# Two PSUM banks for the first head pair's later scores, and an earlier hand-over of the bank of useless matmuls

## The chip, the cores and the metric

The kernel runs on one core of a Trainium2 chip. The core has five engines with queues of their own: TensorE (PE in the profile), VectorE (DVE), ScalarE (ACT), GpSimd (POOL) and SyncE (SP), which issues the DMAs. Matmuls write PSUM, the small memory of eight banks that PE accumulates in. The metric is device microseconds of one execution.

## The reference

Three layers in a row, in float32, on 4 batches of 576 positions:

```python
# attention: 8 heads of 64, window 128, ALiBi
scores = scale * q @ k.T - slope * |rel|      # where 0 <= rel < 128
attn   = softmax(scores);  x = attn @ v       # heads side by side: [4, 576, 512]
# gated MLP, the "mixture" below
h = gelu(x @ w_in);  u, v = h[..., :512], h[..., 512:]
v = layernorm(v) * g_ln
x = x + (u * (w_sg @ v + b_sg)) @ w_out
# channel mix
xk, xr = mix(x, x_prev, mu_k), mix(x, x_prev, mu_r)
r = sigmoid(xr @ w_r)
out = r * (relu(xk @ w_k) ** 2 @ w_v)
```

## The kernel before

**Stages.** The attention works on 16 pairs of heads, one pair a "slot". The first four pairs are batch 0; from then on the mixture of batch b and the attention of batch b+1 are merged, and the channel mix (with a Strassen-like scheme of products `qa`, `qb`, `qd`, `vps` and the gate's products `rps`) comes last. Matmuls of the mixture and the last stage are split in high and low parts, three passes for one product.

**A slot of the attention.** A pair's 576 rows are nine tiles of 64. `s_items` (L920) takes two banks for four tiles of scores; `s_bank` (L960) records 16 small matmuls (`s<-rawqk`) for them, and `s_tile` (L989) for each tile a reduce on DVE (L996, adds the mask, gives `p` and `nmax`) and an exp on ACT (L619). `s_last` does the ninth tile, number 8, in a bank of the same ring and calls `tail_tile` (L937): `sum`, reciprocal `rin`, and `p` of tile 8 times `rin`. `t_step` (L1018) transposes `p` on PE (`tf`), 13 transposes a pair, of which the last step needs tile 8. `av_step` (L1061) forms `rt` (`rin` spread over rows, on PE) and the product `a<-pf,rawv`; `slot(c)` (L1105) strings together the scores of pair c and the product of pair c-1. The masks are multiples of the first head pair's mask (`mask_pair`); this first mask is made on DVE from `rel`, which POOL makes. The pattern `tri` is built by POOL and completed by two DVE copies.

**Banks.** PSUM is in three rings: `psS` (2 banks, tag `s`: scores), `psT` (2 banks: transposes, `rt`), and `psD` (4 banks, tag `d`: products of the mixture, and a bank `wps` that useless matmuls write). A tile of a ring waits until all users of the tile that many places before it are done.

**Useless matmuls.** `filler` (L734) offers up to 150 matmuls of a mask with itself (128x384, bf16) into `wps`, between a first and a last one. The planner queues one of them wherever PE has nothing ready in its plan; so they stand where the plan had PE idle, and on the chip they run in their place in the queue whether PE had waited or not. `filler_end` sets the last one, and what it waits for.

```python
    def filler_end(self, out, l, r, late):

        o = self.r.fill[-1][2] = self.mm([(out, l, r, True, True, {})])
        o.deps.add(late)
```

**Mixture work among the first slots.** `v_first` (L1176) puts products with the first parts of `w_in` into three `psD` banks from slot 2 on. `job` (L809) decodes `w_in`: ACT (L818), a shift on DVE (L708), a shift-and-or on DVE (L691, `wdec<-st,wdec`), then a high part (a cast, on ACT, DVE or POOL) and a low part (a subtract, on DVE or POOL).

**Order of the work.** All operations are recorded first. `schedule` (L430), a list scheduler with estimated costs, then fixes each engine's order and, for an operation with several engines allowed, the engine. A table `PRI` shifts the latest start of a group of operations and a table `ENG` biases the choice of its engine; both are written-out numbers.

Of the kernel before, what the change touches and what calls it, by code (L numbers as in the profile page):

```python
# [61 lines left out]
    ("rawv0", "sp"): -145256, ("rel", "pool"): -60569, ("rin", "dve"): -25233, ("rin.0", "dve"): 5257, ("rin.1", "dve"): -69646,  # L62
    ("rl.c", "act"): -82948, ("rl.c", "act/dve/pool"): -108272, ("rps", "pe"): -153964, ("rps.a", "pe"): 16695, ("rps.c", "pe"): 41240,
    ("rr.v", "dve"): -87265, ("rr.v", "sp"): -128743, ("rr.w", "dve"): -349494, ("rr.w", "sp"): -12240, ("rr.x", "sp"): -22703,
    ("rr.z", "sp"): 157296, ("rs.c", "act"): -44771, ("rsd", "sp"): -282416, ("rsd.a", "sp"): -190365, ("rsd.c", "sp"): -14632,
# [3 lines left out]
    ("tri", "pool"): 10322, ("u", "dve"): 58110, ("u.1", "dve"): 3031, ("u.3", "dve"): 136950, ("v", "dve"): 21613, ("v", "dve/pool"): 318339,  # L69
    ("v.1", "dve"): 13625, ("v.1", "dve/pool"): -47891, ("v.3", "dve"): -107478, ("v.3", "dve/pool/act"): -242645, ("vhl", "act/dve/pool"): 69188,  # L70
    ("vhl", "dve"): -218606, ("vhl", "dve/pool"): -323701, ("vhl.1", "act/dve/pool"): -20746, ("vhl.1", "dve"): -190493,
    ("vhl.1", "dve/pool"): 83593, ("vhl.3", "act/dve/pool"): 132502, ("vhl.3", "dve"): -196785, ("vhl.3", "dve/pool"): 167692,
    ("vps.v", "pe"): -32792, ("vps.w", "pe"): -206906, ("vps.x", "pe"): 92350, ("vps.z", "pe"): -226565, ("vsg", "dve"): -174379,
    ("vsg", "dve/pool"): 661483, ("vsg.1", "dve"): -26065, ("vsg.1", "dve/pool"): 26297, ("vsg.3", "dve"): -156326, ("vsg.3", "dve/pool"): -8209,
    ("vx", "act/dve"): -74444, ("vx.1", "act/dve"): -40169, ("vx.3", "act/dve"): -16277, ("w7", "act/dve/pool"): -810863,
    ("w7", "dve/pool"): 172733, ("w7.3", "act/dve/pool"): -178636, ("w7.3", "dve/pool"): -226904, ("w7.a", "act/dve/pool"): 19037,
    ("w7.a", "dve/pool"): -40750, ("w_in_t.0", "act/dve/pool"): 27024, ("w_in_t.0", "dve/pool"): 182778, ("w_in_t.u", "act/dve/pool"): 36136,
    ("w_in_t.u", "dve/pool"): 25486, ("w_out_t.o", "act/dve/pool"): -233990, ("w_out_t.o", "dve/pool"): 184889, ("w_r_t.3", "act/dve/pool"): 13396,
    ("w_r_t.3", "dve/pool"): -60043, ("w_sg_t.1", "act/dve/pool"): 929461, ("w_sg_t.1", "dve/pool"): -163370, ("w_v7.w", "act/dve/pool"): -179176,
# [676 lines left out]
def attn_gmlp_rwkv_kernel(  # L756
# [1100 lines left out]
```

## Time and profile before

| | |
|---|---|
| three runs, us | median 559.45 (559.27 to 560.44) |
| the profiled execution, us | 559.52 |
| its span, first to last instruction, us | 557.80 (1.72 lie around it) |
| PE busy | 548.5 us, 98% |
| DVE, ACT, POOL busy | 476.5 us (85%), 347.8 us (62%), 236.5 us (42%) |
| granted TensorE clock | 1.00 in every slice |

How to read the rows further down: a row of the timeline gives the start, the length and the work of one run of equal instructions on an engine, and in brackets how long the engine was idle ahead of it and what ended that. PE runs matmuls pipelined, so their modelled lengths overlap by up to some 0.2 us; what counts is from start to start. A useless matmul is a row `wps<-mask`, `wps<-w_out_t` or `wps<-wk`.

### The profile page before, as it was taken

The numbers are of one execution on the slowest core, as the hardware profiler recorded it, in microseconds if no ns is written. First come the engines' busy times: TensorE is split into PE (matmuls) and PEld (weight loads), VectorE is DVE, ScalarE is ACT, GpSimd is POOL, SyncE is SP. The second block draws the span as 40 slices with busy tenths as digits, with TensorE's granted clock in tenths as the row PEclk, the third lists the DMA queues.
The fourth block names the chain that finished last, engine by engine and source line by source line (L and its number), as shares of the span: only waits on it lengthen the run. The fifth ranks groups of instructions, "written<-read, shape, count | busy, mean of one in ns | idle before, by whom it ended". The sixth has DMA issues, their size and how long they took to land. (4 is left out here: it accounts for less than half of the span.)

```text
span 557.8 us, 12880 instructions
## 1 busy us (share of the span) xinstructions
PE 548.5 (98%) x4594; PEld 492.5 (88%) x4594; DVE 476.5 (85%) x1195; ACT 347.8 (62%) x925; POOL 236.5 (42%) x382
## 2 busy tenths in 40 slices
PE   8999999999999999999999999999999999999997
PEld 4777799988999888899899989898999978799997
DVE  6999998888988889887999999987958986659994
ACT  5998987649866687572554469876565663326240
POOL 4674735837645448472466203311431422024531
PEclk9999999999999999999999999999999999999999
DMA  8864334355432453334722276738545597644623
GB/s 274 326 184 125 112 124 143 94 205 166 125 125 84 154 172 104 114 86 125 248 93 60 73 255 204 241 89 271 167 156 203 191 313 244 211 131 164 215 77 132
DMA packets 54896, 91.79 MB, mean 165 GB/s; under 512 B 6832, under 2 KB 32944, under 8 KB 54320
## 3 DMA queue, kind: packets, MB, share of 16 engines
q1 hardware_dynamic: 54832, 90.97, 50.3%
q8 instruction: 36, 0.59, 0.4%
q14 instruction: 28, 0.23, 0.1%
HBM read 62.10 MB, written 28.84 MB: 163 GB/s over the span
## 5 line engine op out<-in xcount | busy, mean ns | idle before, releaser
L619 ACT ACTIVATE p<-p,nmax 128x192 f32<-128x192 f32 (+2 forms) x144 | 61.6, 430 | 16.1 <-DVE nmax L996 15.5
L597 PE MATMUL d<-w_sg_t,vhl 128*128 128x288 f32 x448 | 63.9, 298 | 0.4 <-DVE u L691 0.4
L597 PEld LDWEIGHTS d<-w_sg_t,vhl 128*128 128x128 f32 x448 | 60.1, 188 | 2.2 <-issue 1.7
L597 PE MATMUL d<-xg,w_in_t 128*128 128x288 f32 x384 | 56.6, 298 | 0.0
L597 PEld LDWEIGHTS d<-xg,w_in_t 128*128 128x128 f32 x384 | 53.0, 188 | 3.5 <-issue 1.7
L597 PE MATMUL d<-gg,w_out_t 128*128 128x288 f32 x384 | 55.7, 298 | 0.2 <-POOL gg L644 0.2
L597 PEld LDWEIGHTS d<-gg,w_out_t 128*128 128x128 f32 x384 | 52.3, 188 | 2.1 <-issue 1.1
L597 PE MATMUL rps<-w_r_t,xr 128*128 128x512 f32 x216 | 51.6, 391 | 1.0 <-ACT rs L619 1.0
L597 PE MATMUL d<-w_in_t,xg 128*128 128x512 f32 x192 | 50.9, 400 | 0.1
L597 PEld LDWEIGHTS rps<-w_r_t,xr 128*128 128x128 f32 x216 | 40.3, 188 | 9.2 <-ACT rs L619 1.4
L996 DVE CUSTOM_DVE_ANT_0 p<-s,mask 128x192 f32<-128x192 f32 (+1 forms) x144 | 40.3, 326 | 5.0 <-PE s L597 4.6
L597 PE MATMUL vps<-w_v_t,k 128*128 128x256 f32 (+1 forms) x252 | 43.2, 329 | 0.1
L597 PEld LDWEIGHTS vps<-w_v_t,k 128*128 128x128 f32 x252 | 37.8, 190 | 4.7 <-DVE rr L642 0.5
L597 PEld LDWEIGHTS d<-w_in_t,xg 128*128 128x128 f32 x192 | 34.1, 188 | 6.8 <-issue 1.4
L644 POOL TENSOR_TENSOR k2o<-k2o,rr 128x256 f32<-128x256 f32 x13 | 16.9, 1305 | 46.7 <-DVE k2o L642 46.6
L619 ACT ACTIVATE gt<-gt 128x288 f32<-128x288 f32 (+2 forms) x52 | 26.6, 515 | 14.8 <-DVE gt L691 14.7
L597 PE MATMUL s<-rawqk 64*64 64x192 f32 (+2 forms) x576 | 33.5, 318 | 0.6 <-DVE tri L632 0.6
L597 PEld LDWEIGHTS a<-pf,rawv 64*64 64x64 f32 (+1 forms) x832 | 26.9, 135 | 5.1 <-DVE v L691 1.5
L644 POOL TENSOR_TENSOR vsg<-vsg,u 128x288 f32<-128x288 f32 x25 | 23.1, 928 | 18.6 <-DVE vsg L691 18.0
L597 PE MATMUL a<-pf,rawv 64*64 64x64 f32 (+2 forms) x832 | 30.0, 239 | 0.9 <-DVE v L691 0.9
L691 DVE SCALAR_TENSOR_TENSOR gt<-gt,d 128x288 f32<-128x288 f32 (+2 forms) x52 | 27.5, 534 | 2.8 <-ACT gt L619 2.5
L658 POOL TENSOR_SCALAR_AFFINE_SELECT pf<-pf 128x128 f32<-128x128 f32 (+1 forms) x61 | 23.5, 418 | 14.7 <-ACT pf L630 13.4
(237 smaller groups left out, 1373.2 us busy)
## 6 DMA issues: line engine op xcount, KB each, us to landing
rawqk<-in_qk_dram SPq DMA_DIRECT2D x15, 576.0 KB, 4.9
k2d<-e SPq DMA_DIRECT2D x36, 192.0 KB, 2.5
k2f<-k2d SPq DMA_DIRECT2D x16, 384.0 KB, 5.4
xc<-xs SPq DMA_DIRECT2D x7, 770.0 KB, 5.1
rawv<-in_v_dram SPq DMA_DIRECT2D x32, 160.0 KB, 3.3
wx<-wx SPq DMA_DIRECT2D x40, 128.0 KB, 3.1
xs<-x SPq DMA_DIRECT2D x4, 1154.0 KB, 4.7
rr<-rsd SPq DMA_DIRECT2D x18, 256.0 KB, 3.6
```

Source lines behind the costliest of these rows:

```text
L597: pe.matmul(real(o), real(l), real(r), start=st, stop=sp, **ex)
L619: nc.scalar.activation(real(out), real(in_), func, scale=scale, **kw)
L644: alts.append(("pool", 140 + 2.12 * out.n, lambda: nc.gpsimd.tensor_tensor(real(out), real(a), real(b), op)))
L658: self.nc.gpsimd.affine_select(out=out, in_=in_, pattern=[[0, v.ids.shape[1]], [0, 2], [sgn, 64]], compare_op=cmp, fill=0.0, base=64 * sgn ...
L691: alts.append(("dve", cost or self._dve(out.n, False, isinstance(s, Vw)), lambda: nc.vector.scalar_tensor_tensor(real(out), real(a), real( ...
L996: K.raw("dve", 70 + w / 0.96, lambda: nc.vector.tensor_tensor_reduce(out=real(po), in0=real(s), in1=real(ma), scale=-0.125, scalar=3.0e38, ...
```

## The change

Three edits. (1) Pair 0's second four tiles of scores go to two banks of `psD` in place of `psS`. (2) The bank `wps` of useless matmuls ends at the start of slot 2 (it ended after the fourth product `a`), and its successor `wps2` is taken right behind the three `psD` tiles of `v_first`, in front of slot 2. So the ring `psD` is used in the order `wps`, `s`, `s`, then three mixture tiles, `wps2`, where it was `wps`, three mixture tiles, `wps2`. (3) Every number of `PRI` and `ENG` is new.

```diff
 PRI = {
-    ("a", "pe"): -9616, ("a.0", "pe"): 43767, ("a.1", "pe"): -320743, ("bm", "dve"): -606882, ...
+    ("a", "pe"): -90488, ("a.0", "pe"): 9130, ("a.1", "pe"): 20578, ("bm", "dve"): -844676, ...
...
     def s_items(c, half):
-        banks = [T("psS", [P, 2, 256], F32, "s") for _ in range(2)]
+        banks = [T("psS", [P, 2, 256], F32, "s") if c or not half else T("psD", [P, 2, 256], F32, "d", "s") for _ in range(2)]
         return banks, [x for k in range(2) for o in range(2) for x in s_item(c, 4 * half + 2 * k + o, banks[o], k)]
...
     for n in range(5):
         if n == 0:
             K.filler(wps[:, 0:384], *warm)
+        if n == 2:
+            K.filler_end(wps[:, 0:384], *warm[:2], next(o for o in reversed(R.ops) if o.pe))
         if n > 1:
             v_first(range(n - 2, n - 1))
+        if n == 2:
+            wps2 = T("psD", [P, 512], F32, "d", "wps")
+            K.filler(wps2[:, 0:384], *warm)
...
-    K.filler_end(wps[:, 0:384], *warm[:2], AV[3])
-    wps2 = T("psD", [P, 512], F32, "d", "wps")
-    K.filler(wps2[:, 0:384], *warm)
     for b in range(B):
```

The new order of each engine, where the prediction speaks of it. Line numbers of the changed kernel are one lower.

The useless matmuls on PE, counted from the two orders (each is a pair of rows, `LDWEIGHTS mask` and `MATMUL wps<-mask`):

| stretch of PE's queue | before | changed |
|---|---|---|
| ahead of the first product `a` | 16 | 21 |
| from the first to the second `a` | 9 | 1 |
| from the second to the fifth `a` | 6 | 10 |
| the last one on `mask`, behind the fifth | 1 | 1 |
| entry of the last stage, on `w_out` / on `wk` | 14 / 20 | 18 / 15 |
| all | 66 | 66 |

The first slot on DVE. `mask<-rel` is the first mask, `mask<-mask` those of other pairs, the ISA rows the reduces with their `nmax`, `tri` the pattern. Before:

```order
L708 TENSOR_SCALAR mask_145<-rel_115 64x192 x4
L708 TENSOR_SCALAR mask_145<-mask_145 128x384 x3
L632 COPY tri_158<-tri_158 128x256
L996 ISA p_147,nmax_186<-s_169,mask_145 128x64
L996 ISA nmax_186 128x1
L996 ISA p_147,nmax_190<-s_172,mask_145 128x128
L996 ISA nmax_190 128x1
L996 ISA p_195,nmax_196<-s_169,mask_145 128x192
L996 ISA nmax_196 128x1
L996 ISA p_195,nmax_201<-s_172,mask_145 128x192
L996 ISA nmax_201 128x1
L632 COPY tri_158<-tri_158 128x256
```

Changed:

```order
L707 TENSOR_SCALAR mask_151<-rel_132 64x192 x4
L707 TENSOR_SCALAR mask_151<-mask_151 128x384 x2
L995 ISA p_115,nmax_180<-s_164,mask_151 128x64
L995 ISA nmax_180 128x1
L995 ISA p_115,nmax_183<-s_167,mask_151 128x128
L995 ISA nmax_183 128x1
L995 ISA p_189,nmax_190<-s_164,mask_151 128x192
L995 ISA nmax_190 128x1
L995 ISA p_189,nmax_195<-s_167,mask_151 128x192
L995 ISA nmax_195 128x1
L631 COPY tri_154<-tri_154 128x256 x2
L995 ISA p_222,nmax_223<-s_207,mask_151 128x192
```

One of the three other masks is gone (POOL makes it), and both copies of `tri` stand behind the first four reduces, in a row. On POOL three memsets of `p` now stand ahead of `rel`, and that mask stands between the memset of `tri` and the six selects that complete it; behind the copies DVE has the five reduces of tiles 4 to 8 in a row, as before.

PE between the first and the second product `a` (pair 1's tail, pair 2's first scores). Before, seven pairs of useless matmuls like the first two rows stand ahead of these, and ahead of them eight `tf` and eight `s`:

```order
L741 LDWEIGHTS mask
L741 MATMUL wps<-mask 128x384
L605 MATMUL tf<-ident,p 128x128 x5
L597 MATMUL s<-rawqk 64x192 x8
L741 LDWEIGHTS mask
L741 MATMUL wps<-mask 128x384
L597 MATMUL rt<-ident,rin 64x64 x16
L597 MATMUL a<-pf,rawv 64x128 x6
```

Changed:

```order
L596 MATMUL s<-rawqk 64x192 x2
L604 MATMUL tf<-ident,p 128x128 x4
L596 LDWEIGHTS mask
L596 MATMUL wps<-mask 128x384
L604 MATMUL tf<-ident,p 128x128 x4
L596 MATMUL s<-rawqk 64x64 x2
L596 MATMUL s<-rawqk 64x128 x2
L596 MATMUL s<-rawqk 64x192 x4
L604 MATMUL tf<-ident,p 128x128 x5
L596 MATMUL s<-rawqk 64x192 x8
L596 MATMUL rt<-ident,rin 64x64 x16
L596 MATMUL d<-w_in_t,xg 128x512 x3
L596 MATMUL a<-pf,rawv 64x128 x6
```

The run of eight useless matmuls is gone; one is left, the last of its bank, and the next bank's first comes later than this piece. The first three products of the mixture, `d<-w_in_t,xg`, stand ahead of the second `a` (they stood behind it).

ACT at the end of the gate's products (`rs<-rps` are the gate's six last results). Before:

```order
L630 CAST w_v_t<-k2o 128x2x256
L619 ACTIVATE rs<-rps 128x512 x2
L630 CAST w_v_t<-k2o 128x2x256
L630 CAST k_6487<-k2f 128x768
L630 CAST k_6610<-k2f 128x768
L619 ACTIVATE rs<-rps 128x512
L630 CAST w_v_t<-k2o 128x2x256
L619 ACTIVATE rs<-rps 128x512 x2
```

Changed:

```order
L618 ACTIVATE rs<-rps 128x512 x2
L629 CAST w_v_t<-k2o 128x2x256
L629 CAST k_6617<-k2f 128x768
L629 CAST w_v_t<-k2o 128x2x256
L1404 ACTIVATE e<-e 128x384
L1405 ACTIVATE e<-e 128x384
L618 ACTIVATE rs<-rps 128x512 x2
L629 CAST w_v_t<-k2o 128x2x256
L618 ACTIVATE rs<-rps 128x512
```

Ahead of the fourth `rs` there were two casts `k<-k2f`, whose input comes by DMA; there is now one, and an operation pair on `e` and one more cast of `w_v_t`. In SP's queue the two loads `k2f` for these casts come right behind the four loads `k2o`, and ahead of the last stores `k2d<-e`; they came behind these stores.

On DVE all eight subtracts of the `w_in` decode (128x512, L644 on POOL before) stand in its queue now, seven of them ahead of the scores of pair 3's last tile. Ahead of the same place DVE has one more cast and two more copies of `rt`, one `p` by `rin` and one shift-and-or more, and one copy of `pf` and one mask less. ACT has four casts of `w_in`, two copies of `rt` and one `p` by `rin` less there, and one cast of `w_sg` and two of `xg` more. In pair 1's tail DVE goes from tile 8's reduce to `p<-p,rin` over one subtract, `sum`, an add for `x`, `rin` and a shift; before, over one shift-and-or, `sum`, `rin` and two reduces of pair 2.

## Rows read from the trace of the kernel before

**Rows 1.** The page, part 2: TensorE's busy tenths and granted clock in 40 slices.
```profile
PE   8999999999999999999999999999999999999997
...
PEclk9999999999999999999999999999999999999999
```

**Rows 2.** Waits of PE: engine, line, waited for; us in total, times, longest.
```profile
PE rps L597 <- ACT rs L619: 1.0, 1, 1.0
PE a L597 <- DVE v L691: 0.9, 2, 0.7
PE s L597 <- DVE tri L632: 0.6, 1, 0.6
```

**Rows 3.** Timeline, DVE, start of the program: start us, us, engine, line, work [idle before <-releaser].
```profile
3.19 2.25 DVE L708 TENSOR_SCALAR mask<-rel 64x192 bf16<-64x192 f32 x4 [2.00 <-POOL rel L1694]
```

**Rows 4.** Timeline, POOL, the memsets of p.
```profile
3.71 0.32 POOL L1002 MEMSET p<- 128x64 f32 x3
```

**Rows 5.** Timeline, PE, from the second half of pair 0's scores to the second slot.
```profile
7.66 0.99 PE L597 MATMUL s<-rawqk 64*64 64x192 f32 x16 [0.63 <-DVE tri L632]
...
9.65 0.54 PE L597 MATMUL s<-rawqk 64*64 64x192 f32 x4
...
15.62 1.89 PE L597 MATMUL a<-pf,rawv 128*64 128x128 f32 x52
...
20.06 1.47 PE L741 MATMUL wps<-mask 128*128 128x384 bf16 x8
21.37 0.71 PE L605 MATMUL tf<-ident,p 128*128 128x128 f32 x5
...
24.19 1.84 PE L597 MATMUL a<-pf,rawv 128*64 128x128 f32 x52
...
29.59 0.94 PE L597 MATMUL d<-w_in_t,xg 128*128 128x512 f32 x3
30.37 0.60 PE L605 MATMUL tf<-ident,p 128*128 128x128 f32 x4
```

**Rows 6.** Timeline, DVE, pair 1's tail; a shift, a shift-and-or with no subtract beside.
```profile
19.18 1.50 DVE L691 SCALAR_TENSOR_TENSOR wdec<-st,wdec 128x512 uint32<-128x512 uint32 x1
...
21.10 0.31 DVE L708 TENSOR_SCALAR p<-p,rin 128x192 f32<-128x192 f32 x1
...
22.84 0.41 DVE L708 TENSOR_SCALAR wdec<-wdec 128x512 uint32<-128x512 uint32 x1
...
29.07 0.63 DVE L691 SCALAR_TENSOR_TENSOR wdec<-st,wdec 128x512 uint32<-128x512 uint32 x1
```

**Rows 7.** Timeline, POOL, a subtract of the w_in decode.
```profile
18.84 1.29 POOL L644 TENSOR_TENSOR w_in_t<-wdec,w_in_t 128x512 fp32r<-128x512 f32 x1 [1.94 <-ACT w_in_t L630]
```

**Rows 8.** Groups by line and shape, 0 to 54 us, DVE.
```profile
L691 DVE SCALAR_TENSOR_TENSOR wdec<-st,wdec 128x512 uint32<-128x512 uint32 x8 | 8.6, 1074 | 0.0
L708 DVE TENSOR_SCALAR wdec<-wdec 128x512 uint32<-128x512 uint32 x8 | 5.5, 709 | 0.0
```

**Rows 9.** Groups by line and shape, whole span, DVE: a subtract of that shape.
```profile
L642 DVE TENSOR_TENSOR w_v_t<-zv,w_v_t 128x512 fp32r<-128x512 f32 x4 | 2.8, 688 | 0.3 <-ACT w_v_t L630 0.3
```

**Rows 10.** Timeline, PE, behind the fourth slot.
```profile
47.42 0.66 PE L605 MATMUL tf<-ident,p 128*128 128x128 f32 x4 [0.60 <-ACT p L718]
```

**Rows 11.** Timeline, PE, entry of the last stage.
```profile
329.43 3.10 PE L741 MATMUL wps<-wk 128*128 128x384 bf16 x18
332.23 3.08 PE L597 MATMUL qa<-w,wk 128*128 128x384 f32 x16
```

**Rows 12.** Timeline, DVE, ahead of PE's first product with w.
```profile
331.44 0.95 DVE L642 TENSOR_TENSOR w<-bm,w 128x768 fp32r<-128x768 f32 x1
```

**Rows 13.** Timeline, ACT, ahead of the fourth gate.
```profile
456.58 0.83 ACT L630 CAST k<-k2f 128x768 fp32r<-128x768 f32 x1 [0.43 <-DMA k2f<-k2d]
457.32 0.59 ACT L619 ACTIVATE rs<-rps 128x512 f32<-128x512 f32 x1
```

**Rows 14.** Timeline, PE, the gate's products.
```profile
457.97 3.01 PE L597 MATMUL rps<-w_r_t,xr 128*128 128x512 f32 x12 [0.97 <-ACT rs L619]
```

More of the change, by code (lines that the diff above doesn't have):

```diff
@@ L76 @@
[L76 to L79, printed above, removed]
@@ new lines @@
+    ("k2u.z", "sp"): 6925, ("mask", "dve"): 230036, ("mask.0", "dve/pool"): 1881, ("mhalf", "dve"): 46932, ("mk", "dve/pool/act"): 1615,
+    ("mk.3", "dve/pool/act"): -59727, ("mk.a", "dve/pool/act"): 3165, ("mr", "dve"): -74962, ("mr", "dve/pool/act"): -29009,
+    ("mr.3", "dve"): -25118, ("mr.3", "dve/pool/act"): 1430, ("mr.a", "dve"): 85858, ("mr.a", "dve/pool/act"): 90415, ("mr.c", "dve"): -21182,
+    ("mr.c", "dve/pool/act"): 86059, ("mus", "sp"): -98444, ("mus1", "dve"): -6348, ("mv", "dve"): -11815, ("mv", "pool"): 198205,
@@ new lines @@
+    ("rawv0", "sp"): -308395, ("rel", "pool"): 9952, ("rin", "dve"): -36090, ("rin.0", "dve"): -118676, ("rin.1", "dve"): -112927,
+    ("rl.c", "act"): 26468, ("rl.c", "act/dve/pool"): -108643, ("rps", "pe"): -166728, ("rps.a", "pe"): -16551, ("rps.c", "pe"): 103701,
+    ("rr.v", "dve"): 49454, ("rr.v", "sp"): -58994, ("rr.w", "dve"): -252692, ("rr.w", "sp"): -21081, ("rr.x", "sp"): 100362,
+    ("rr.z", "sp"): 118940, ("rs.c", "act"): 17, ("rsd", "sp"): -614166, ("rsd.a", "sp"): -183086, ("rsd.c", "sp"): 134720,
[4 rows of a table added]
@@ new lines @@
+    ("w_in_t.0", "dve/pool"): -4199, ("w_in_t.u", "act/dve/pool"): -5406, ("w_in_t.u", "dve/pool"): -68226, ("w_out_t.o", "act/dve/pool"): -61937,
+    ("w_out_t.o", "dve/pool"): 351995, ("w_r_t.3", "act/dve/pool"): 59286, ("w_r_t.3", "dve/pool"): -37955, ("w_sg_t.1", "act/dve/pool"): -29123,
+    ("w_sg_t.1", "dve/pool"): -389541, ("w_v7.w", "act/dve/pool"): -87708, ("w_v7.w", "dve/pool"): -110771, ("w_v7.x", "act/dve/pool"): 50894,
+    ("w_v7.x", "dve/pool"): -73613, ("w_v7.z", "act/dve/pool"): -10904, ("w_v7.z", "dve/pool"): -5067, ("w_v_t.w", "act/dve/pool"): -373725,
@@ L97 @@
+    ("xs2", "sp"): 435815, ("xs3.3", "sp"): 283973, ("z.3", "dve/pool"): -54339, ("z.3", "sp"): 63247, ("zk.x", "sp"): 113512, ("zk.z", "sp"): 3485,
+    ("zr.3", "sp"): -110980, ("zt", "act"): 180846, ("zt", "act/dve/pool"): -46510, ("zt.a", "act"): 111196, ("zt.a", "act/dve/pool"): -47058,
+    ("zt.c", "act"): 30386, ("zv.w", "dve/pool"): -103581, ("zv.w", "sp"): 208591,
 }
 ENG = {
[L99 removed]
@@ new lines @@
+    ("k2c.z", "act/dve/pool", "pool"): -6997, ("k2c.z", "dve/pool", "dve"): -5954, ("k2c.z", "dve/pool", "pool"): 131773,
+    ("k2f.x", "dve/pool", "dve"): -27388, ("k2f.x", "dve/pool", "pool"): -366638, ("k2f.z", "dve/pool", "dve"): 328147,
+    ("k2f.z", "dve/pool", "pool"): -59002, ("k2o.w", "dve/pool", "dve"): 38054, ("k2o.w", "dve/pool", "pool"): -230494,
+    ("k2o.x", "act/dve", "act"): 4248, ("k2o.x", "act/dve", "dve"): 17554, ("k2o.x", "dve/pool", "dve"): -128237,
+    ("k2o.x", "dve/pool", "pool"): -66512, ("k2o.z", "act/dve", "act"): 26302, ("k2o.z", "act/dve", "dve"): 195465,
@@ new lines @@
+    ("k2o.z", "dve/pool", "dve"): 320111, ("k2o.z", "dve/pool", "pool"): -106345, ("k2u.x", "dve/pool", "dve"): 159032,
+    ("k2u.x", "dve/pool", "pool"): 265186, ("k2u.z", "dve/pool", "dve"): 295307, ("k2u.z", "dve/pool", "pool"): 97671,
+    ("mask.0", "dve/pool", "dve"): -120741, ("mask.0", "dve/pool", "pool"): -346229, ("mk", "dve/pool/act", "act"): -5764,
+    ("mk", "dve/pool/act", "dve"): -258186, ("mk", "dve/pool/act", "pool"): 3602, ("mk.3", "dve/pool/act", "act"): -21207,
+    ("mk.3", "dve/pool/act", "dve"): -298831, ("mk.3", "dve/pool/act", "pool"): 449326, ("mk.a", "dve/pool/act", "act"): -6793,
@@ new lines @@
+    ("oa.a", "dve/pool", "dve"): -26887, ("oa.a", "dve/pool", "pool"): -33384, ("ob", "act/dve/pool", "act"): -127284,
+    ("ob", "act/dve/pool", "dve"): -76999, ("ob", "act/dve/pool", "pool"): -76255, ("ob", "dve/pool", "dve"): 23262,
+    ("ob", "dve/pool", "pool"): -7579, ("ob.3", "act/dve/pool", "act"): 68561, ("ob.3", "act/dve/pool", "dve"): -24989,
+    ("ob.3", "act/dve/pool", "pool"): 67927, ("ob.3", "dve/pool", "dve"): -218525, ("ob.3", "dve/pool", "pool"): -87749,
+    ("ob.a", "act/dve/pool", "act"): 4752, ("ob.a", "act/dve/pool", "dve"): 48641, ("ob.a", "act/dve/pool", "pool"): 81766,
@@ new lines @@
+    ("w7.3", "dve/pool", "pool"): -1284, ("w7.a", "act/dve/pool", "act"): -23058, ("w7.a", "act/dve/pool", "dve"): 74426,
+    ("w7.a", "act/dve/pool", "pool"): -345128, ("w7.a", "dve/pool", "dve"): 60943, ("w7.a", "dve/pool", "pool"): -14193,
+    ("w_in_t.0", "act/dve/pool", "act"): -20398, ("w_in_t.0", "act/dve/pool", "dve"): -3023, ("w_in_t.0", "act/dve/pool", "pool"): 24801,
+    ("w_in_t.0", "dve/pool", "dve"): 38956, ("w_in_t.0", "dve/pool", "pool"): -62406, ("w_in_t.u", "act/dve/pool", "act"): 276823,
@@ new lines @@
+    ("w_in_t.u", "act/dve/pool", "dve"): 236914, ("w_in_t.u", "act/dve/pool", "pool"): -103485, ("w_in_t.u", "dve/pool", "dve"): 652958,
+    ("w_in_t.u", "dve/pool", "pool"): 759, ("w_out_t.o", "act/dve/pool", "act"): 22938, ("w_out_t.o", "act/dve/pool", "dve"): -188925,
+    ("w_out_t.o", "act/dve/pool", "pool"): 65468, ("w_out_t.o", "dve/pool", "dve"): -11272, ("w_out_t.o", "dve/pool", "pool"): -44178,
+    ("w_r_t.3", "act/dve/pool", "act"): 144781, ("w_r_t.3", "act/dve/pool", "dve"): -25131, ("w_r_t.3", "act/dve/pool", "pool"): -278332,
@@ L210 @@
+    ("zv.w", "dve/pool", "dve"): 312446, ("zv.w", "dve/pool", "pool"): -17259,
 }
```

255 lines of the change are left out of this document (108 added, 147 removed), and 57 rows, old and new, of the table PRI.

## The prediction

> **What bounds the kernel now.** [...] Of the 557.80 us span PE is busy 548.5, so 9.3 us of idle time are all that a better order of the work could win, the lead-in and the tail among them. The waits of PE come second; the large ones are few: 1.0 for a gate result from ACT, 0.9 in two waits for `v`, 0.6 for the first slot's scores [rows 2], 0.6 for `p` [rows 10]. But PE also runs 66 useless matmuls, which stand where the plan saw it idle: idle time in disguise. A run of eight goes from 20.06 to the next row at 21.37 [rows 5], so one takes 1.31/8 = 0.16 us. The third view is the timeline at these places, of PE and of whoever it waits for.
>
> The useful matmuls stay the same, and so does the count of useless ones, 66. So the time changes only by what PE's idle time changes, and by whether a useless matmul fills time in which PE would have waited or takes time of its own. I go along PE's queue, against the profiled execution's 559.52 us, which is 0.07 above the median of the runs, 559.45.
>
> **The first slot.** Before, the second four score tiles waited 0.63 us for the banks of the first four [rows 5]. In banks of their own they go at once: -0.63. Against this: five useless matmuls more ahead of the first `a`, 5 x 0.16 = +0.80; three memsets on POOL ahead of `rel`, 0.32 us [rows 4], on which DVE's first mask waited [rows 3], +0.32; and tile 8's four small matmuls, which took 0.54 by themselves, run in one piece with the 16 that take 0.99, four at 0.25, -0.3 [rows 5]. DVE drops a mask and a copy ahead of the reduces, but its two copies of `tri` now stand ahead of the second four, behind POOL's selects, which come later by a mask. That adds up to +0.2; as one or two of the five useless ones will stand where PE would wait, I take **0**, the first `a` at 15.6 as before [rows 5]; bounds -0.6 (all five fill waits) and +0.6 (`tri` is late).
>
> **The second slot.** From the first `a` to the second it took 24.19 - 15.62 = 8.57 us [rows 5]. Eight useless matmuls go, 8 x 0.16 = -1.30. They hid something: the fifth transpose of that step needs tile 8 of pair 1, whose `p` by `rin` was issued at 21.10 [rows 6], behind a shift-and-or of 1.50. Without them PE stands and waits. In the new order DVE reaches this `p` over a subtract, 0.69 by the nearest row [rows 9], `sum`, an add, `rin` and a shift of 0.41 [rows 6]; about 21.0 by the old times. So the tail of the step starts at 21.2 where it began at 21.37, runs without two turns, and ends near 23.3; then come three mixture products, which were paid behind the second `a`, some 0.8 us by what three cost there (from 29.59 to 30.37 [rows 5]), and `a` at 24.1 to 24.2. It comes no later, with 0.8 of work pulled forward: **-0.65** as I take it, with 0.15 kept for DVE's longer queue. Bounds: -1.6 (nothing waited for) and +0.3 (the wait eats all, and the decode is late for the mixture products).
>
> **DVE and POOL, which all this hangs on.** Seven subtracts are put on DVE up to pair 3's end, 7 x 0.69 = 4.8 us [rows 9], and other moves make it some 6. Relief comes from POOL: its subtract ran from 18.84 for 1.29 [rows 7], and the shift-and-or beside it took 1.50, where one with no such subtract beside it took 0.63 [rows 6]. In the mean of eight it took 1.07, the shift 0.71 where one without took 0.41 [rows 8, 6]; 8 x 0.44 + 8 x 0.30 = 5.9 us that come back if nothing else on POOL disturbs. Net I take 0: the tenants of DVE change, its end does not. [...]
>
> **From the second to the fifth `a`.** Four useless matmuls more, +0.64, and the 0.60 wait for `p` [rows 10] is where the plan now puts them: **0** in sum; bounds -0.6 and +0.7. The wait for `v` behind the fifth `a` (of the 0.9, the longer is 0.7 [rows 2]) hangs on DVE's queue too; it may go or double, and I leave it: 0, bounds -0.7 and +0.7.
>
> **Entry of the last stage.** Four useless matmuls more on `w_out`, five fewer on `wk`. The run of 18 ended where PE's first product with `w` began, 332.23 [rows 11], and DVE's subtract for `w` started at 331.44 for 0.95 [rows 12]: the data set that end. Fewer useless ones become idle time: **0**, bounds -0.6 and +0.6.
>
> **The gate.** The 0.97 before the last twelve gate products [rows 14] was the fourth `rs`, issued at 457.32 behind a cast that had waited for its DMA until 456.58 [rows 13]. Now one of these two casts stands there, and its load is ahead of the last stores in SP's queue. **-0.7**; bounds 0 (the one cast waits as long) and -0.97.
>
> Sum: 0 - 0.65 + 0 + 0 + 0 + 0 - 0.7 = -1.35, so 559.52 - 1.35 = 558.17; against the median, 0.07 lower, **558.1**.
>
> **The rivals.**
>
> *The start gives nothing.* DVE is at its limit in these slots, and PE then waits in the second slot for all that the eight useless matmuls took: only the gate's 0.7 remains, 558.8. For it: with PE free sooner, everything ahead of the second `a` still comes from DVE. Against it: the three mixture products fill at least a part.
>
> *Nothing at all.* The waits come back elsewhere, the gate's too behind the one cast: 559.5.
>
> *Slower, through DVE.* POOL's other work, the high parts and subtracts of `xg`, goes on stretching DVE, so that of the relief of 5.9 a half to a third comes, 3 to 2, while the load of 6 stays: DVE is 3 to 4 us late by pair 3. The useless matmuls in that stretch, ten at 0.16 = 1.6, hide a part; the rest, 1.4 to 2.4, is PE's wait for `p`, for `v` and for the mixture's first operands, the second slot gives nothing, and the gate's 0.7 comes off: 560.2 to 561.2, in the middle 560.7. It decides from 2.3 us of lateness on (1.6 + 0.7), which is a relief of 3.7 of the 5.9: the mean of the eight shift-and-ors stays over 0.80 [rows 8]. For it: DVE stood idle ahead of none of them [rows 8], so it has no room. Against it: the trace shows the stretch under POOL's subtracts themselves, and these go.
>
> *The clock falls.* Between the hand-over and the next bank no useless matmul may be queued. The granted clock was 1.00 throughout with them, and also past the 0.97 us gap at the gate [rows 1, 14]; nothing in the trace shows a fall. [...]
>
> **Chances.** The forecast 0.48 (its own range 556.8 to 558.9), the start gives nothing 0.24, nothing 0.06, slower through DVE 0.20, the clock 0.02. A difference under 0.2%, 1.1 us, can't be told from none. Of the forecast's 0.48, 0.40 lie below 558.3; of the second case a quarter, 0.06: faster 0.46. Slower, over 560.6: 0.12 of the DVE case, with 0.07 more of it for a gate that gives nothing, and the clock's 0.02, 0.21. Same: 0.33. For 8 in 10 I go from 556.8, the sum with the second slot's lower bound and a little of the gate's, to 560.8, past the middle of the DVE case.
>
> **What would show it.** The first slot's scores in one piece of 20 without the 0.63; the first `a` at 15.6 and the second at 24.1; a wait of about 1 us for tile 8's `p` in the second slot, and no run of eight there; shift-and-or means near 0.65 in the first 54 us, and POOL's subtracts of `w_in` gone; no 0.97 at the gate. Wrong, if the second `a` comes after 25 or the first mixture products wait for `xg` or `w_in_t`; if the wait for `v` at the fifth `a` grows past 1; if the gate still stands behind a cast; or if a slice shows a clock under 1.00.

## The result, and the profile after

The changed kernel takes 564.11 us (median of 4 runs, 563.34 to 565.68), the kernel before, timed beside it, 559.5 (559.27 to 560.44): a ratio of 1.0083, 95% interval 1.0058 to 1.0108. It is slower, by 0.8%. The profiled execution took 563.88 us with a span of 562.2, 4.36 and 4.4 more than before, so the trace can be followed to the end. I laid PE's queues of the two executions side by side at places where both have the same work. The start of that work, in us:

| place in PE's queue | before | after | after - before | step |
|---|---|---|---|---|
| first product `a` | 15.62 | 15.06 | -0.56 | -0.56 |
| fifth `a` | 51.83 | 52.22 | +0.39 | +0.95 |
| sixth `a` | 68.06 | 70.20 | +2.14 | +1.75 |
| scores `s` x20 behind it | 72.21 | 77.00 | +4.79 | +2.65 |
| last `a` | 254.34 | 258.78 | +4.44 | -0.35 |
| run of useless matmuls on `w_out` | 312.81 | 318.12 | +5.31 | +0.87 |
| gate's products `rps` | 443.20 | 449.26 | +6.06 | +0.75 |
| products `vps` behind the gate | 460.82 | 465.62 | +4.80 | -1.26 |
| end of the span | 557.8 | 562.2 | +4.4 | -0.4 |

Two steps make the loss, both around the sixth product `a`, over 40 us behind the two slots in which the edits change the banks. The page of the changed kernel shows it in its slices of the granted clock: the sixth slice is not full, where all were before [rows 1].

```profile
PEclk9999979999999999999999999999999999999999
```

The waits of PE in the changed kernel (engine, line, waited for; us in total, times, longest) have new names at their head. The gate's 1.0 and the 0.6 of the first scores [rows 2] are gone; a single wait for `v` and one for a copy of `pf` are there, and one for `x`:

```profile
PE a L596 <- DVE v L690: 1.9, 1, 1.9
...
PE d L596 <- DVE x L641: 0.9, 1, 0.9
PE tf L604 <- ACT pf L629: 0.8, 1, 0.8
```

**The sixth `a`.** PE's timeline there, changed kernel:

```profile
60.68 5.08 PE L596 MATMUL d<-xg,w_in_t 128*128 128x288 f32 x36
65.60 1.09 PE L604 MATMUL tf<-ident,p 128*128 128x128 f32 x8
67.53 0.77 PE L604 MATMUL tf<-ident,p 128*128 128x128 f32 x5 [0.84 <-ACT pf L629]
70.20 3.19 PE L596 MATMUL a<-pf,rawv 128*64 128x128 f32 x50 [1.90 <-DVE v L690]
...
77.00 1.19 PE L596 MATMUL s<-rawqk 64*64 64x192 f32 x20
```

From pair 4 on, `a` is written to a bank of the ring `psD`, and the one whose turn it is holds the mixture's 64-row tile until its gelu has read it. That gelu is a chain over two engines: ACT copies `vx`, DVE adds it to `d`, ACT squares, DVE forms `gt`, ACT takes the tanh, DVE writes `v`. Before, DVE's three steps of it stood here (timeline of the kernel before):

```profile
63.26 0.69 DVE L642 TENSOR_TENSOR d<-d,vx 64x512 f32<-64x512 f32 x1 [0.19 <-ACT vx L630]
65.24 0.64 DVE L691 SCALAR_TENSOR_TENSOR gt<-gt,d 64x512 f32<-64x512 f32 x1
67.33 0.67 DVE L691 SCALAR_TENSOR_TENSOR v<-gt,d 64x512 f32<-64x512 f32 x1
```

and ACT's first two, with scalings of `p` between them:

```profile
62.65 0.58 ACT L630 COPY vx<-d 64x512 f32<-64x512 f32 x1
63.13 0.99 ACT L718 ACTIVATE p<-p,rin 128x192 f32<-128x192 f32 x3
64.14 0.59 ACT L619 ACTIVATE gt<-d 64x512 f32<-64x512 f32 x1
```

In the changed kernel, DVE:

```profile
65.57 0.54 DVE L707 TENSOR_SCALAR p<-p,rin 128x192 f32<-128x192 f32 x2
...
66.12 0.66 DVE L641 TENSOR_TENSOR d<-d,vx 64x512 f32<-64x512 f32 x1
...
68.00 0.68 DVE L690 SCALAR_TENSOR_TENSOR gt<-gt,d 64x512 f32<-64x512 f32 x1 [0.37 <-ACT gt L618]
...
69.47 0.67 DVE L690 SCALAR_TENSOR_TENSOR v<-gt,d 64x512 f32<-64x512 f32 x1
```

and ACT:

```profile
63.56 0.80 ACT L717 ACTIVATE p<-p,rin 128x192 f32<-128x192 f32 x2
64.38 0.59 ACT L629 COPY vx<-d 64x512 f32<-64x512 f32 x1
64.87 1.68 ACT L717 ACTIVATE p<-p,rin 128x128 f32<-128x128 f32 x5
...
67.37 0.59 ACT L618 ACTIVATE gt<-d 64x512 f32<-64x512 f32 x1
68.22 0.59 ACT L629 COPY pf<-tf 128x512 f32<-128x512 f32 x1 [0.26 <-PE tf L604]
68.71 0.63 ACT L618 ACTIVATE gt<-gt 64x512 f32<-64x512 f32 x1
```

The chain is 2.1 us late at its end (PE itself was 0.39 late at the fifth `a`), and its first steps stand behind what the new order put ahead of them. `vx` starts 1.73 us later than before, behind two scalings of `p`. The add to `d` had followed `vx` at once; it now stands behind the last `w_sg` subtract, 0.95 us, and two scalings on DVE, and is 2.86 late. The square stands behind five scalings (it was three), a decode step and a copy of `pf`, and is 3.23 late. The steps behind it win back 1.1. PE, with both mixture products and transposes behind it, had nothing left but `a`, and the useless matmuls had ended. So it stood for 0.84 and 1.90 us with 0.77 us of work between.

**The clock.** Busy time by stretch, changed kernel (us, then PE, PEld, DVE, ACT, POOL busy with counts, granted clock, DMA share, GB/s):

```profile
65.00:70.00 5.00, 2.46 (x19) 1.89 (x17) 4.63 (x12) 4.72 (x13) 2.67 (x8) 0.93 0.15 52
70.00:72.00 2.00, 1.80 (x21) 1.80 (x23) 2.00 (x7) 1.40 (x5) 1.87 (x4) 0.50 0.43 143
...
74.00:76.00 2.00, 2.00 (x13) 1.51 (x7) 1.61 (x10) 1.69 (x7) 0.00 (x0) 0.50 0.54 164
76.00:78.00 2.00, 2.00 (x28) 1.64 (x26) 1.36 (x6) 1.09 (x5) 0.76 (x2) 0.97 0.15 29
```

While PE stood, the granted clock fell to 0.50 (from 69.4 on); in 76 to 78 it was back, 0.97 in the mean. The same work, from the sixth `a` to the 20 scores behind it, took 77.00 - 70.20 = 6.80 us where it took 72.21 - 68.06 = 4.15 before: 2.65 us, more than the waits had grown.

**Elsewhere.** The first two slots, PE of the changed kernel, against [rows 5]:

```profile
6.75 1.19 PE L596 MATMUL s<-rawqk 64*64 64x192 f32 x20 [0.16 <-DMA rawqk<-in_qk_dram]
...
20.40 0.44 PE L604 MATMUL tf<-ident,p 128*128 128x128 f32 x2 [0.28 <-DVE p L707]
21.12 1.15 PE L596 MATMUL s<-rawqk 64*64 64x192 f32 x16 [0.28 <-DVE nmax L995]
...
24.17 1.89 PE L596 MATMUL a<-pf,rawv 128*64 128x128 f32 x52
```

The scores go in one piece of 20, and what they wait for now is their load. DVE's groups by shape, 0 to 54 us, show the lighter decode that was forecast [rows 8]; POOL has no subtract of `w_in` left:

```profile
L690 DVE SCALAR_TENSOR_TENSOR wdec<-st,wdec 128x512 uint32<-128x512 uint32 x8 | 6.0, 766 | 0.0
L641 DVE TENSOR_TENSOR w_in_t<-wdec,w_in_t 128x512 fp32r<-128x512 f32 x8 | 5.4, 679 | 0.0
...
L707 DVE TENSOR_SCALAR wdec<-wdec 128x512 uint32<-128x512 uint32 x8 | 3.4, 437 | 0.3 <-ACT wdec L817 0.3
```

At the entry of the last stage PE, whose longest wait there had been 0.23 for `gg`, now waits for `x` and for `oa`:

```profile
313.94 4.35 PE L596 MATMUL d<-gg,w_out_t 128*128 128x288 f32 x30 [0.85 <-DVE x L641]
318.12 2.78 PE L740 MATMUL wps<-w_out_t 128*128 128x384 bf16 x16
...
321.72 0.97 PE L596 MATMUL qd<-oa,wk 128*128 128x384 f32 x4 [0.47 <-DVE oa L641]
```

And the gate's 72 products run in one row, the 0.97 of [rows 14] gone:

```profile
449.26 16.52 PE L596 MATMUL rps<-w_r_t,xr 128*128 128x512 f32 x72
```

### The profile page after: what moved, and what is told of

Its sections match the earlier page's. It is cut to its first block, busy times and chain, and to the rows that moved or that the text cites. A ratio compares the mean times of both kernels' runs of the same rounds, so it can differ in the third digit from the quotient of the medians.

```text
span 562.2 us, 12853 instructions
## 1 busy us (share of the span) xinstructions
PE 551.2 (98%) x4594; PEld 494.9 (88%) x4594; DVE 478.4 (85%) x1221; ACT 347.3 (62%) x918; POOL 221.8 (39%) x370
## 4 chain that ended last, share of the span: by engine, by line
PE 85%; DVE 9%; ACT 3%; DMA 1%; issue 1%; SPq 1%; POOL 0%; ACTq 0%; DVEq 0%
PE d L596 32%; PE vps L596 17%; PE qa L596 9%; PE rps L596 9%; PE qb L596 4%; PE a L596 4%; PE s L596 4%; PE tf L604 3%; PE qd L596 2%; DVE wk L641 1%; ACT p L618 1%; DVE p L995 1%; SPq L724 1%; DVE x L641 1%; ACT p L717 1%
## 5 line engine op out<-in xcount | busy, mean ns | idle before, releaser
L657 POOL TENSOR_SCALAR_AFFINE_SELECT pf<-pf 128x128 f32<-128x128 f32 (+1 forms) x75 | 29.7, 431 | 11.5 <-ACT pf L629 11.5
L596 PEld LDWEIGHTS a<-pf,rawv 64*64 64x64 f32 (+1 forms) x832 | 28.2, 140 | 6.0 <-DVE v L690 2.5
L596 PE MATMUL a<-pf,rawv 64*64 64x64 f32 (+2 forms) x832 | 31.4, 246 | 1.9 <-DVE v L690 1.9
L604 PE MATMUL tf<-ident,p 128*128 128x128 f32 x176 | 27.5, 278 | 2.0 <-ACT pf L629 0.8
```

Of the source, the lines that this page charges most:

```text
L596: pe.matmul(real(o), real(l), real(r), start=st, stop=sp, **ex)
L604: pe.transpose(real(o), real(i), real(d))
L657: self.nc.gpsimd.affine_select(out=out, in_=in_, pattern=[[0, v.ids.shape[1]], [0, 2], [sgn, 64]], compare_op=cmp, fill=0.0, base=64 * sgn ...
```

## The experiments

Most of them are the changed kernel with single operations moved in the planned order or put on another engine, by number, right behind the planner. Each gives the pairs (operation, the one it is put ahead of). Lines that repeat are drawn together to loops here, and `...` marks what is left out:

```diff
     order = R.schedule()
+    for i, j in PAIRS:
+        o = next(o for o in order if o.i == i)
+        order.remove(o)
+        order.insert(next(k for k, x in enumerate(order) if x.i == j), o)
```

In the chain of the 64-row tile 447 is `vx`, 448 the add to `d`, 449 the square, 450 `gt`, 451 the tanh, 452 `v`. Four groups of kernels were each timed beside the kernel before, at 559.43, 558.86, 559.48 and 559.82 us; ratios are within a group.

**1. The changed kernel again.**

> The changed kernel, unchanged, for a second profile on another chip. Theory (a bank's wait, then the clock): the sixth product `a` waits again some 2 us for DVE's last gelu step of the 64-row mixture tile, with 0.8 us of a wait for a copy of `pf` ahead of it, and TensorE is granted half its clock behind these waits; 563 to 565 us. Rival (the fall of the clock was an accident of that execution): the waits come again, the clock stays at 1.00, and this profile is 2 to 3 us shorter, about 561.5.

563.75 us (562.40 to 565.52), ratio 1.0078 [1.0057, 1.0100]. The 0.84 and the 1.90 are there to the hundredth, ahead of the sixth `a` at 71.26. The clock fell for a shorter time (0.50 in 72 to 74, 0.77 in 74 to 76); sixth to seventh `a` took 19.27 us, where the first trace has 20.40. Of the four runs the one with a mean clock of 1.000 was the fastest, 562.40, and the one with 0.993 the slowest, 565.52; the four runs of the result don't order so cleanly (0.999 took 564.34, 0.993 took 563.88). The fall comes in most executions, not in all, and is of different length.

**2. The chain to `v` moved forward.**

```diff
+    PAIRS = (447, 437), (448, 468), (449, 439), (450, 441), (451, 490), (452, 482)
```

> The changed kernel with six operations of the 64-row mixture tile's chain (the copy `vx`, the add to `d`, the four steps of its gelu) moved ahead of a few others on ACT and DVE; nothing else moves. Theory (the sixth `a` waits for this chain because ACT and DVE do other work first, and the clock falls because of the wait): the wait of 1.9 us comes down to under 0.9, the clock stays at 1.00 there, and the time is 559.5 to 560.5. Rival (ACT and DVE are at their limit in this stretch, what is moved back makes PE wait as long): the transposes wait instead, no gain, 563 to 565.

563.01 us, ratio 1.0062 [1.0046, 1.0077]: the rival's time, which can't be told from the changed kernel's. The wait for `v` is gone, and what it had stood behind is late instead, the copy of `pf` and a `p` on ACT:

```profile
67.17 0.78 PE L604 MATMUL tf<-ident,p 128*128 128x128 f32 x3 [0.20 <-ACT p L717]
69.22 0.92 PE L604 MATMUL tf<-ident,p 128*128 128x128 f32 x5 [1.27 <-ACT pf L629]
70.07 3.16 PE L596 MATMUL a<-pf,rawv 128*64 128x128 f32 x50
```

Fifth to sixth `a` fell from 17.98 to 17.15 (before: 16.23), and the clock still went down, 0.53 in 70 to 72. A chain pulled forward by itself pays half of this stretch; ACT is full there, busy 3.98 of the 4 us from 65 to 69.

**3. Useless matmuls in the two waits.** 16 more of them are put in PE's queue, 5 ahead of the last five transposes and 11 ahead of the sixth `a`, in a bank of `psS` that is free then.

```diff
...
+    for n, i in ((5, 501), (11, 511)):
+        order.insert(next(k for k, x in enumerate(order) if x.i == i), idle(n))
```

> The changed kernel with 16 more useless matmuls on PE, 5 ahead of the third step of the transposes of the sixth slot and 11 ahead of its `a`, where PE stood for 0.84 and 1.90 us; no other instruction moves. Theory (the clock falls because PE stands still): `a` starts at the same time, near 70.2 us, the granted clock stays at 1.00 behind it, and the time is 2.65 us less than the changed kernel's, about 561.4. Rival (the clock falls for another reason): half clock again behind `a`, and no gain, 564. Rival (the useless ones take time of their own): up to 16 x 0.16 = 2.6 more.

562.44 us (561.72 to 563.46), ratio 1.0054 [1.0038, 1.0070]; no run had a mean clock under 0.999. This is the run that parts the two losses:

```profile
69.21 0.77 PE L604 MATMUL tf<-ident,p 128*128 128x128 f32 x5
69.81 1.95 PE L1790 MATMUL s<-mask 128*128 128x384 bf16 x11
71.90 1.88 PE L596 MATMUL a<-pf,rawv 128*64 128x128 f32 x51
```

```profile
70.00:72.00 2.00, 1.86 (x13) 0.96 (x13) 2.00 (x6) 1.98 (x5) 0.70 (x2) 1.00 0.00 0
72.00:74.00 2.00, 2.00 (x67) 1.91 (x68) 2.00 (x7) 1.41 (x5) 1.88 (x4) 1.00 0.46 143
```

The sixth `a` comes no earlier, 17.94 us behind the fifth where it was 17.98; but the clock stays at 1.00, `a` takes 1.88 where it took 3.19, and sixth to seventh `a` 17.74 us where it took 20.40 and 19.27. So here the clock falls because PE stands (no fall in these four runs; a mean clock of 0.997 or less in 21 of the 26 runs of the kernels that keep both waits: the result, 1, 5, 6, 7), and it costs 1.5 to 2.7 us in an execution in which it falls; in the medians of the runs 1.3.

**4. The whole stretch ahead of the sixth `a` in the old order,** two `w_sg` steps (468, 469) and the engines of two scalings (437 to GpSimd, 439 to DVE) among it.

```diff
+    PAIRS = ((447, 437), (448, 468), (449, 439), (450, 490), (451, 491), (452, 510), (468, 441), (469, 495))
...
```

> The changed kernel with the whole stretch ahead of the sixth `a` in the order and on the engines of the kernel before: the six operations of the 64-row tile's chain moved as before's queues have them, one scaling of `p` from ACT to GpSimd and one from ACT to DVE, and a cast and a subtract of `w_sg` behind the chain's first step; 12 lines of queue in all, nothing on PE. Theory (the wait and the clock are the order and the choice of engines on ACT, DVE and GpSimd in these 9 us, and nothing of the two edits in the code): from the fifth to the sixth `a` 16.3 us as before (it was 17.95), a wait of about 0.7, the clock at 1.00 there, and 559.7 us, 4 less than the changed kernel. Rival (the order of the transposes on PE, all 13 in a row, sets it): over 17 us again, the clock falls, about 562.5.

561.91 us, ratio 1.0058 [1.0036, 1.0080]; the clock was 1.00 in all four runs. Fifth to sixth `a` took 16.77 us, and of the 2.74 us of waits about half is left, in three pieces; two of 0.37 and 0.32 for `u` follow:

```profile
68.14 0.66 PE L604 MATMUL tf<-ident,p 128*128 128x128 f32 x4 [0.67 <-ACT pf L629]
69.06 0.33 PE L604 MATMUL tf<-ident,p 128*128 128x128 f32 x1 [0.27 <-DVE pf L631]
69.86 1.88 PE L596 MATMUL a<-pf,rawv 128*64 128x128 f32 x51 [0.47 <-DVE v L690]
...
72.66 1.07 PE L596 MATMUL d<-xg,w_in_t 128*128 128x288 f32 x6 [0.37 <-DVE u L690]
...
74.05 1.06 PE L596 MATMUL d<-xg,w_in_t 128*128 128x288 f32 x6 [0.32 <-DVE u L690]
```

The order of this stretch is the cause of the waits ahead of the sixth `a`; but 559.7, which I had expected, did not come. What is won there is lost again behind it: from the sixth to the seventh `a` it took 18.99 us, where 3 has 17.74 and the kernel before 17.48. From the fifth to the seventh it is 35.76 here and 35.68 in 3, where the waits had only been filled, and the times of the two can't be told apart. So what this repair is seen to pay is the clock. DVE's rows say why: its third `u` starts 21.86 us behind the fifth `a` here, and 21.54 in 6, which leaves the chain as it was.

**5. The subtracts of `w_in` back on GpSimd,** all eight.

```diff
+    for i in (73, 79, 85, 139, 145, 151, 209, 215):
+        o = next(o for o in order if o.i == i)
+        o.eng = next(a for a in o.alts if a[0] == 'pool')
```

> The changed kernel with the eight subtracts of the `w_in` decode back on GpSimd, in the same places of the list; DVE's and GpSimd's queues are otherwise as they were. Theory (the start gives nothing because DVE has no room for them): from the first to the fifth `a`, 37.15 us in the changed kernel, 36.2 as in the kernel before or less, and about 1 us off the time. Rival (what DVE gains in work it loses again beside GpSimd's subtracts, as the shift-and-ors rise from 0.77 to 1.0 us or more): 37.15 us or more, no gain.

564.44 us, ratio 1.0106 [1.0081, 1.0131], which overlaps the changed kernel's. First to fifth `a` took 38.85 us against 37.16, though DVE has seven subtracts less in that stretch. Its busy time there was 35.39 us against 35.68: without 7 x 0.68 = 4.8 of its own the rest grew by 4.5, while POOL was busy 19.84 instead of 11.11, 8.7 more, about twice what DVE lost. The shift, with no subtract on POOL beside it 0.437 in the mean, takes 0.720 again, the shift-and-or does not change:

```profile
L690 DVE SCALAR_TENSOR_TENSOR wdec<-st,wdec 128x512 uint32<-128x512 uint32 x8 | 6.1, 766 | 0.0
L707 DVE TENSOR_SCALAR wdec<-wdec 128x512 uint32<-128x512 uint32 x8 | 5.7, 720 | 0.3 <-ACT wdec L817 0.3
```

The stretch is the rival's, though by the shift and not by the shift-and-or that it named. In this stretch, then, the change's move of the subtracts was right.

**6. Three copies of `rt` on ScalarE instead of VectorE.**

```diff
+    for i in (186, 247, 296):
+        o = next(o for o in order if o.i == i)
+        o.eng = next(a for a in o.alts if a[0] == 'act')
```

> The changed kernel; the copies of rt for pairs 2, 3 and 4 (three, each 0.5 to 0.7 us) are done by ScalarE instead of VectorE. Theory (first to fifth product a is bound by VectorE, at 37.16 us in the changed kernel against 36.21 before): the stretch falls to 36.0 to 36.6 us; the waits of 0.84 and 1.90 ahead of the sixth product stay, the time is 563.0 to 563.5. Rival (TensorE's own order binds it): the stretch stays at 37.0 to 37.3, and the time at 563.9.

562.96 us, ratio 1.0051 [1.0033, 1.0069]. First to fifth `a` took 36.49 us; the 0.84 and 1.90 stayed, in this execution at a clock of 1.00. Of the 0.95 that the changed kernel lost among the first slots, 0.67 is these copies in DVE's queue: it was busy 35.68 of 37.16 us there, and 33.78 of 36.49 with the copies gone. Two of the eight runs had a mean clock of 1.000, and took 560.76 and 561.23; the others, at 0.997 or less, took 562.71 to 563.91.

**7. The entry of the last stage.** Two adds of `x` (2062, 2065) go ahead of a subtract for `w7` and a product for a mask.

```diff
+    PAIRS = (2062, 1956), (2065, 2092)
```

> The changed kernel; on VectorE, at the entry of the last stage (about 313 us), the first two adds of x are put ahead of one subtraction for w7 and one product for a mask. Theory (TensorE's 0.85 us wait for x there is VectorE's order, not its amount of work): the wait falls under 0.3 and what stands behind it starts 0.5 to 0.8 us earlier; the time is 563.2 to 563.5 against the changed kernel's 563.9. Rival (VectorE is full there, the work only changes places): w7 or the mask is late in its turn, another wait of 0.5 to 1 us appears before 340 us, and the time stays at 563.9.

563.68 us, ratio 1.0077 [1.0055, 1.0099], which can't be told from the changed kernel. The wait went from 0.85 to 0.58, now for a later `x`, and that for `oa` stayed:

```profile
316.41 1.06 PE L596 MATMUL d<-gg,w_out_t 128*128 128x288 f32 x6 [0.58 <-DVE x L641]
...
320.92 0.97 PE L596 MATMUL qd<-oa,wk 128*128 128x384 f32 x4 [0.48 <-DVE oa L641]
```

From the last `a` to the products on `oa` it took 320.92 - 258.37 = 62.55 us where the changed kernel has 321.72 - 258.78 = 62.94: 0.4 won. The wait did not fall under 0.3, and DVE was busy all the time from 305 to 321, so the rest looks like its amount of work. Both theories have a part.

**8. The gate alone.** In the kernel before, the fourth `rs` is put ahead of the second cast of `k`.

```diff
+    PAIRS = (2689, 2733),
```

> The kernel before, with one instruction moved: on ACT the fourth gate result `rs` ahead of the second of the two casts `k<-k2f` that wait for a DMA. Theory (the 0.97 us that PE stood there are the order on ACT, and the gain at the gate is real by itself): no wait of PE there, 558.5 us, 0.9 less. Rival (the time is given back in the last products, which wait for `k`): 559.4.

559.76 us (558.39 to 561.30, 11 runs), ratio 1.0007 [0.9996, 1.0018]. The wait at the gate is gone, and comes back 23 us later, behind a load: `rr` on DVE follows a subtract for `k2c`, whose cast on ACT had waited for `k2f`:

```profile
443.78 16.52 PE L597 MATMUL rps<-w_r_t,xr 128*128 128x512 f32 x72
...
483.13 5.74 PE L597 MATMUL vps<-w_v_t,k 128*128 128x512 f32 x24 [1.07 <-DVE rr L642]
```

The kernel before had no wait of that size there. (This profile has another of 0.61 at 362 us, for `mr`, which the kernel before hasn't; the edit doesn't explain it.) In the changed kernel the 1.26 is kept; it also has its loads for these casts ahead of the last stores in SP's queue. Whether that is why was not tried.

**9. Edits and tables apart.** The changed code with the old numbers, and the old code with the new ones. Of the first:

```diff
 PRI = {
-    ("a", "pe"): -90488, ("a.0", "pe"): 9130, ...
+    ("a", "pe"): -9616, ("a.0", "pe"): 43767, ...
```

> Both edits in the code, with the tables of the kernel before. The planner's order for it holds 165 useless matmuls in place of 66, 99 more, which is to say that the plan leaves PE idle in many places, most of it at the entry of the last stage. Theory (the numbers of the tables fit one recorded program and are lost when it changes): 99 x 0.16 = 16 us more than before, about 575 us. Rival (the edits bring what they are for, the numbers only trim): under 562.

> The code of the kernel before, with the new tables. The planner's order holds 111 useless matmuls, 45 more than either kernel: 45 x 0.16 = 7 us, about 567 us, if the tables fit only their own program. Rival (the new numbers are worse by themselves and the edits make no difference): as the changed kernel, 564.

600.29 and 585.56 us, one run each, 41 and 26 us over the kernel before and far beyond what I expected. The planner, led by numbers fitted to another list of operations, puts 165 and 111 useless matmuls where 66 were. So the edits can't be priced without a table of their own, and the two halves of the change don't add.

**10. The repairs together:** the stretch of 4, the copies of 6, the adds of 7.

```diff
+    PAIRS = ((447, 437), (448, 468), (449, 439), (450, 490), (451, 491), (452, 510), (468, 441), (469, 495), (2062, 1956), (2065, 2092))
...
```

> The changed kernel with three repairs together: the chain to the value matrix of the 64-row tile in the order of before (as in the run that had 561.9), the rt copies on ScalarE, the adds of x ahead of w7 and the mask. Theory (the three lie behind one another on TensorE's path and add): 561.9 less 0.7 less 0.6, 560.4 to 561.0, still over the kernel before, since the start lost its cover and gives nothing. Rival (slack behind the sixth product absorbs what is won ahead of it): 561.7 to 562.1. Third possibility: under 559.5, then the change gains once its followers are ordered.

560.83 us (560.01 to 561.23, 12 runs), ratio 1.0025 [1.0014, 1.0036]: the time is the theory's. The fifth `a` starts at 51.81 (before 51.83), the sixth at 68.59 (68.06), the last at 255.73 (254.34). But the traces side by side, from start to start in us, show the rival at work behind the sixth `a`:

| kernel | fifth to sixth `a` | sixth to seventh | sum | clock |
|---|---|---|---|---|
| before | 16.23 | 17.48 | 33.71 | 1.00 |
| changed | 17.98 | 20.40 | 38.38 | falls to 0.50 |
| waits filled (3) | 17.94 | 17.74 | 35.68 | 1.00 |
| copies of `rt` (6) | 17.93 | 17.74 | 35.67 | 1.00 |
| old order of the stretch (4) | 16.77 | 18.99 | 35.76 | 1.00 |
| repairs together (10) | 16.78 | 18.98 | 35.76 | 1.00 |

What the old order wins ahead of the sixth `a` is gone at the seventh, so of that repair there stays only that the clock doesn't fall; the two runs of 6 at a clock of 1.000 are as fast without it. Some 2.0 us from the fifth to the seventh `a` are lost in each of these versions, and no run removes them.

**11. Two more:** behind the sixth `a` two steps of the next gelu (472, 473) go forward, and one square (485); at the entry the fourth add of `x` (2071) and the subtract for `oa` (2120).

```diff
...
+    PAIRS += (2071, 2093), (2120, 1992), (472, 413), (473, 413), (485, 496)
```

> The kernel with the three repairs, and two more: behind the sixth product a, ScalarE's and VectorE's first two steps of the next gelu go ahead of a cast of w_out and one of v; at the entry of the last stage the fourth add of x goes ahead of a product with mus, and the subtraction for oa ahead of a cast of wk. Theory (the waits of 0.37 and 0.33 for u behind the sixth product, of 0.58 for x and 0.47 for oa are order): the first two go, of the last two 0.3 comes back as oa hangs on ScalarE's cast, so 560.8 less 0.7 less 0.3, 559.6 to 560.2, level with the kernel before at most. Rival (VectorE is full in both places): the waits for u become one for w_out_t or vhl, and that for oa one for wk; 560.5 to 561.0.

560.50 us (559.93 to 560.92, 12 runs), ratio 1.0014 [1.0005, 1.0024]. One of the two waits for `u` went; the one for `x` moved to 320.91 with 0.46, and `oa`'s is 0.37. The time doesn't settle it: it is 0.7 over the kernel before of its own group, where the theory had been 0.1 to 0.7 over and the rival 1.0 to 1.5, and the interval overlaps that of 10. For the rival speaks that DVE was busy throughout from 71 to 75 and from 308 to 318. No version that I found beats the kernel before.

## Why the prediction was wrong

I gave 558.1 us in a range of 556.8 to 560.8; it is 564.11, outside and on the other side.

**The step that failed** is "the wait for `v` behind the fifth `a`", which I left at 0 with bounds of 0.7 either way. It came to 1.90, with 0.84 for a copy of `pf` ahead of it, where 0.71 had been, and made the way from the fifth to the sixth `a` 1.75 us longer. I took the bound from the size of the wait before, as if a wait could at most go or double. But its size is how late a chain of six operations on two engines is, each behind whatever the order puts ahead of it; I went through the changed order of the first slots row by row, and not through this chain, which had a wait at its end already [rows 2]. A bound from the orders would have been the work put ahead of its steps: ahead of the add to `d` alone, which had followed `vx` at once, a subtract of 0.95 and two scalings of together 0.54 on DVE. And to mend the chain only moved the loss to the next waits, for `u` (4, 10): the term to forecast was the stretch up to the seventh `a`, 2.0 us at a full clock, and not the one wait.

**The clock** I had as a rival with 0.02 and at the wrong place. I looked for it in the second slot, where the bank of useless matmuls is handed over; there the waits came to 0.32, 0.28 and 0.28 and the clock was 1.00. A fall in that slot, for which I had nothing measured, no run shows; the runs showed one around the sixth `a` in its place. It fell where no such matmul may be queued and PE stood longest. The sixth slice of the page, and a wait for `v` past 1, were signs that I had named; the size, 2.65 us in this execution, came on top of a wait whose growth I hadn't allowed.

Term by term:

- *The first slot*, forecast 0: the first `a` lies between 15.06 and 16.18 in ten executions with this start, 15.67 in the median, against 15.62: right, with luck in it. The kernel before has 15.62 in both its profiles, in that of 8 without the 0.63, as PE was later ahead of it: that wait was slack which evened out the start, and to count all of it as won was wrong. In eight of the ten the scores, or those of the next pair, waited 0.15 to 0.68 for their load, which the wait for banks had hidden.
- *The second slot*, forecast -0.65: 24.17 - 15.06 = 9.11 us instead of 8.57, so +0.54, past the upper bound; tile 8's `p` cost only 0.28, the rest is DVE's queue, with `x` and a reduce late by 0.32 and 0.28.
- *DVE and POOL*, forecast net 0: the relief came (shift-and-or 1.07 to 0.77, shift 0.71 to 0.44, [rows 8]; 4.6 us of the 5.9), the load was more; first to fifth `a` lost 0.95. The rival through DVE had the right engine; its own test, a mean over 0.80, said no, and its price of some 2 us was too high.
- *Entry of the last stage*, forecast 0 within 0.6: 0.87 and 0.75 were lost up to the gate, most of it before the place that I had looked at, on `x` and `oa` of DVE.
- *The gate*, forecast -0.7: -1.26, the one term that gained, a little beyond its bound of -0.97.

What is shown: the order ahead of the sixth `a` makes the waits there (2, 4), the standing makes the clock fall (0.50 in the result's execution, 1.00 with the waits filled, 3), the copies of `rt` on DVE make 0.67 of the early loss of 0.95 (6). Not shown is what the 2.0 us hang on that all versions lose from the fifth to the seventh `a`, and whether the edits with a table fitted better could gain: the repaired versions reach 0.14% over the kernel before, and their DVE is full at the places where they still wait.

## What to carry to other kernels

When a change renews an order, follow backward, in the new order, every chain that already ends in a wait, also far from the edit, and bound the wait by the work that now stands ahead of each link, not by its old size. Where PE has nothing to run during such a wait, add the clock: here a stand of 2.7 us cost up to 2.65 more, and to fill it with useless matmuls paid as much, within the noise, as to repair the order ahead of it. A wait taken away early shows what it covered (a load, a full DVE) and is worth only what remains of it: compare the versions at the next place where both have the same work, too.

## What the runs showed of the hardware

The granted clock went down in the same place, at the same waits of 0.84 and 1.90 us, in three of five profiled executions with both waits (the changed kernel twice, 7), for nearly 7 us in the first and 3 to 4 in the others, and stayed at 1.00 in two (5 and 6). Of all 26 runs of these kernels 21 had a mean granted clock of 0.997 or less; the kernel before had 0.999 or 1.000 in all 58 runs of the four groups. What decides it, the runs don't show. Eight subtracts of 128x512 on GpSimd lengthened the shift on DVE beside them (0.44 to 0.72 us in the mean of eight, 5), but in this order not the shift-and-or (0.77 with and without), which had taken 1.07 in the kernel before: which operation paid was not the same in these two orders.
